# Slots 1 to 24 of a top-k attention kernel issued in an order from a table, with one small add as a tile and a load of v behind another transfer

## The chip, the cores and the metric

The kernel runs on one core of one Trainium2 chip. The metric is the time of one execution in microseconds (us), as the device measures it. A core has five engines with a queue of instructions each, worked off in order: TensorE (PE; its weight loads are shown apart as PEld), VectorE (DVE), ScalarE (ACT), GpSimd (POOL) and SyncE (SP), which here issues nearly all transfers between HBM and the on-chip memory SBUF. Queues wait for one another through semaphores, which the framework sets from the order in which the program issues its instructions.

## The reference

Attention over 8 batches, 8 heads, 576 tokens and head dimension 64, in which each row of scores keeps its 32 largest values, and then a feed-forward layer with a gated activation:

```
scores = scale * q @ k.T                      # per batch and head: 576 x 576
kth    = 32nd largest of each row
scores = where(scores >= kth, scores, -1e9)
attn   = exp(scores - max)
attn   = attn / (sum(attn) + 1e-9)
x      = attn @ v                             # (8*576) x 512 after joining the heads
h      = x @ w_in                             # 512 -> 2048
out    = (h * sigmoid(1.702 * h)) @ w_out     # 2048 -> 512
```

Inputs of the attention are float32; the two weights come as 64-bit floats and are rounded to float32 on the chip.

## The kernel before, in words

**Slots.** The attention is cut into 144 slots, 18 for each batch. A slot is 128 query rows of two heads: `scores` (L330) multiplies q and k on TensorE in tiles of 64x64; `copy_scores` (L345) brings one copy from the accumulators (PSUM) to SBUF on ScalarE (tile `sc`, four buffers); `pair_up` (L354) writes the larger and the smaller of each pair of scores on VectorE (L360), which frees the accumulators; `topk` (L374) finds the 32 largest by four rounds of MAX8 (L386) and three of MATCH_REPLACE8 (L390) per head on VectorE; `bounds` (L399) makes the cut and the offset on GpSimd; `mask` and `exps` (L418, L428) make the exponentials and their sums `den` on ScalarE; `invert` (L433) adds 1e-9 and takes the reciprocal `rden`. For slots up to 11 (`PAIRED`) the add is a scalar add on VectorE (L439), for later ones on GpSimd (L437).

**From weights to x.** Up to slot 9 the probabilities are turned by TensorE (`divide`, L448, and `turn`, L468 and L471). From slot 10 on `normalize` (L454, GpSimd) divides them, `split` (L490, ScalarE) separates their halves into the buffer `sc`, SyncE writes them to HBM (`rows`, L492) and a transposing transfer brings them back turned (`turn_by_dma`, L498). The next `copy_scores` that uses the same buffer must wait until `rows` is written. `values` and its variants (L526, L557, L586) multiply with v; the result is `x`.

**The feed-forward layer.** Four slots make a block of 128 tokens, 36 in all. A block has four units: `hidden` (L662, TensorE), `tanh` (L678 and L681, ScalarE), `gate` (L690, L691 on GpSimd; L693 on VectorE for the first two blocks), `combine` (L715 to L718, GpSimd) and `project` (L760 for the first two blocks, L776 after). For the first two blocks `hidden` and `project` use tiles of 128x128, after that of 128x64.

**Weights.** In slots 0 to 10 the 32 pieces of the weights are loaded into a ring of seven buffers (`load_piece`, L134) and rounded: ScalarE (L155, L157, L159), a shift on VectorE (L158, 32 times), and two or three passes on GpSimd (L148, L151, L156). The buffers are free for the next loads when the passes are done.

**What sets the order.** It is written out by hand: the program is issued line by line, and each engine works in that order. `opening` starts, `slot(n)` (L949) issues slots 0 to 10, `filling_slot` (L1099) slots 11 to 20, and `steady_pair` (L1175) two slots at a time from 21 on. In all of them a stage of slot n is issued beside later stages of slots before it: the scores of slot n + 2, the search of n, the exponentials of n - 1, the values of n - 2 or n - 3. `filling_slot` issues a `load_v` that is due (one, in slot 20: L210 and L221, the v of the second batch) ahead of the scores, so ahead of the `rows` of that slot on SyncE's queue.

Of the kernel before, what the change touches and what calls it, by code (L numbers as in the profile page):

```python
# [9 lines left out]
ALU = mybir.AluOpType  # L10
ENG = mybir.EngineType
F32 = mybir.dt.float32
# [7 lines left out]
P = 128  # L20
# [9 lines left out]
TO_ZERO = 2.0**-100  # L30


@with_exitstack
def kernel(
    ctx: ExitStack,
# [23 lines left out]

    nc = tc.nc

    B, H, S, D = q.shape
    C = H * D
# [24 lines left out]
    STEADY = PAIRED + 2  # L90
# [5 lines left out]
    const = ctx.enter_context(tc.tile_pool(name="const", bufs=1))  # L96
# [22 lines left out]
    make_identity(nc, ident[:])  # L119
    win = const.tile([P, CC, DFF], F32, name="win")  # L120
    wout = const.tile([P, FC, C], F32, name="wout")

# [170 lines left out]
    def write_all():  # L293
        while writes:
            writes.pop(0)()
# [26 lines left out]
    N = len(slots)  # L322
    PER = N // B
    st = [{} for _ in slots]
# [108 lines left out]
    def invert(n):  # L433

        some = small.tile([P, 2], F32, name="some", tag="sums")
        if n > PAIRED:
            nc.gpsimd.tensor_scalar(some[:], st[n]["den"][:], 1e-9, None, op0=ALU.add)  # L437
        else:
            nc.vector.tensor_scalar_add(some[:], st[n]["den"][:], 1e-9)  # L439
        rden = st[n]["rden"] = small.tile([P, 2], F32, name="rden", tag="inverse")  # L440
        nc.vector.reciprocal(rden[:], some[:])  # L441

# [402 lines left out]
    for n in by_slot:  # L845
        first = sum(map(len, list(by_slot.values())[:n]))
# [60 lines left out]
    def opening():  # L907

        stay_warm(8, v_tail[:, 0, :, :].rearrange("p j d -> p (j d)"))
        load("q", 0, 0, nc.sync)  # L910
        load("k", 0, 0, nc.scalar)
        for hp in range(2):
            for name in "qk":
                if hp:
                    load(name, 0, hp)
        for x in by_slot[0]:
            load_piece(x)
        prepare_first()
# [180 lines left out]
    def filling_slot(n, beside, pool_ahead, behind, pool_behind, late=[]):  # L1099

        todo = later.pop(n, [])
        due = [(fn, args) for fn, args in todo if fn is prepare_by_dma]
        exponentials(n - 1)
        for fn in beside:
            fn()
        for fn in pool_ahead:
            fn()
        find(n, 8)
        for fn, args in todo:
            if fn is load_v:  # L1110
                fn(*args)
        scores(n + 2)
        if n == PAIRED:
            normalize(n - 1)
            split(n - 1)
            copy_scores(n + 2)
        else:
            copy_scores(n + 2)
            normalize(n - 1)
            split(n - 1)  # L1120
        write_all()
        for fn, args in todo:
            if fn not in (prepare_by_dma, load_v):
                fn(*args)
        turn_by_dma(n - 1)
        while turns:
            turns.pop(0)()
        for fn in pool_behind:
            fn()
        bounds(n)  # L1130
        for fn in behind + late:
            fn()
        for fn, args in due:
            fn(*args)
# [106 lines left out]
    def last_units():  # L1241
# [7 lines left out]
        project_one()  # L1249
        leave_all()  # L1250

    with tc.manual_schedule():
# [41 lines left out]
```

## Time and profile before

| | |
|---|---|
| median of 3 runs | 1378.75 us (1377.12 to 1379.25) |
| the profiled execution | 1379.59 us |
| its span, first to last instruction | 1377.8 us |
| mean granted TensorE clock | 0.992 |

Busy time by engine and by stretches of the span, the chain that ended last, and the groups of instructions are views of the same execution. In a row of groups stand line, engine, operation, output and inputs with their shapes, the count, then the busy time and the mean of one instruction, then the idle time of the engine ahead of them with what ended it. A row of instructions in order of time begins with start and length in us. Idle time of an engine costs something only where that engine, or one that waits for it, sets the end.

### The profile page before, as it was taken

What the parts mean: (1) busy time and instruction counts of PE and PEld (TensorE: products, weight loads), DVE (VectorE), ACT (ScalarE), POOL (GpSimd) and SP (SyncE); (2) the same over time, 40 slices, a digit from 0 to 9 for tenths busy, and PEclk for the clock granted to TensorE, in tenths of its full rate; (3) what the DMA queues carried; (4) which work ended last, traced back from release to release, by engine and by line L of the source; (5) the groups of instructions that cost most, each with busy time, mean ns of one, the idle gap of its engine ahead of it and who ended that gap; (6) DMA issues with size and microseconds to landing.
All of it is one profiled execution on the core that took longest, in us unless ns stands there. A gap on an engine that the chain in (4) does not pass through costs nothing.

```text
span 1377.8 us, 54398 instructions
## 1 busy us (share of the span) xinstructions
PE 1341.2 (97%) x22560; PEld 1205.0 (87%) x22560; DVE 1286.0 (93%) x3392; ACT 1164.1 (84%) x1930; POOL 964.4 (70%) x1758
## 2 busy tenths in 40 slices
PE   7789999999999999999999999999999999999998
PEld 5676578899999999999999999999998999999998
DVE  7999998999999999999999999999999999999912
ACT  6988887998889888988898988888888998888841
POOL 3776676777777776777777777677777777777770
PEclk8999999999999999999999999999999999999999
DMA  7551568787889786977898668988888768855640
GB/s 232 155 163 62 151 159 198 179 196 196 205 210 211 178 189 173 232 193 192 192 227 208 182 174 193 210 198 191 197 211 208 195 176 183 184 142 135 151 118 17
DMA packets 527223, 246.92 MB, mean 179 GB/s; under 512 B 458880, under 2 KB 505472, under 8 KB 526976
## 3 DMA queue, kind: packets, MB, share of 16 engines
q1 hardware_dynamic: 526544, 243.16, 71.5%
q8 instruction: 177, 2.90, 0.9%
q14 instruction: 70, 0.57, 0.1%
q10 hardware_dynamic: 432, 0.30, 0.1%
HBM read 46.01 MB, written 103.42 MB: 108 GB/s over the span
## 4 chain that ended last, share of the span: by engine, by line
PE 79%; DMA 3%; ACT 1%; issue 0%; POOL 0%; SPq 0%; DVE 0%; DVEq 0%; ACTq 0%; POOLq 0%
PE ph L662 32%; PE po L776 28%; PE o L586 10%; PE s_ps L339 9%; DMA pt<-rows 2%; DMA rows<-sc 1%; ACT pr L428 0%; ACT sc L418 0%; ACT sc L490 0%; ACT sc L350 0%; ACT halves L268 0%; ACT raws L794 0%; SPq L221 0%; POOL pr L454 0%; ACT h L681 0%
## 5 line engine op out<-in xcount | busy, mean ns | idle before, releaser
L386 DVE MAX8 top<-ranked 128x8 f32<-128x288 f32 (+1 forms) x1152 | 637.6, 596 | 0.0
L662 PE MATMUL ph<-xT,win 128*64 128x128 f32 (+1 forms) x8544 | 493.8, 273 | 0.0
L662 PEld LDWEIGHTS ph<-xT,win 128*64 128x64 f32 (+1 forms) x8544 | 469.4, 137 | 27.6 <-issue 24.1
L390 DVE MATCH_REPLACE8 ranked<-top,ranked 128x288 f32<-128x288 f32 (+1 forms) x864 | 462.4, 543 | 0.0
L490 ACT COPY sc<-pr 128x2304 uint16<-128x2304 uint16 x134 | 283.4, 2115 | 90.1 <-POOL pr L454 90.0
L454 POOL TENSOR_SCALAR pr<-pr,rden 128x576 f32<-128x576 f32 x268 | 197.9, 748 | 49.2 <-DVE rden L441 47.7
L428 ACT ACTIVATE pr<-sc,low 128x576 f32<-128x576 f32 x288 | 219.9, 769 | 0.0
L418 ACT ACTIVATE sc<-sc,cut 128x576 f32<-128x576 f32 x288 | 208.6, 779 | 4.7 <-POOL cut L404 4.7
L360 DVE TENSOR_TENSOR ranked<-s_ps,sc 128x576 f32<-128x576 f32 x286 | 201.8, 747 | 3.8 <-ACT sc L350 3.8
L776 PE MATMUL po<-raws,h 128*64 128x128 f32 x2112 | 205.3, 273 | 0.0
L776 PE MATMUL po<-wout,h 128*64 128x128 f32 x2112 | 205.3, 273 | 0.0
L350 ACT COPY sc<-s_ps 128x576 f32<-128x576 f32 x286 | 168.5, 642 | 26.9 <-PE s_ps L339 14.4
L437 POOL TENSOR_SCALAR some<-den 128x2 f32<-128x2 f32 x132 | 29.3, 222 | 221.6 <-ACT pr L428 221.4
L339 PE MATMUL s_ps<-qk_t 64*64 64x288 f32 x2304 | 177.6, 421 | 5.6 <-DVE ranked L360 4.4
L691 POOL TENSOR_TENSOR th<-th,h 128x512 f32<-128x512 f32 x134 | 171.8, 1282 | 11.2
L776 PE MATMUL po<-wout,th 128*64 128x128 f32 x2176 | 165.3, 273 | 0.0
L776 PEld LDWEIGHTS po<-raws,h 128*64 128x64 f32 x2112 | 133.8, 137 | 0.0
L776 PEld LDWEIGHTS po<-wout,h 128*64 128x64 f32 x2112 | 133.7, 137 | 0.0
L776 PEld LDWEIGHTS po<-wout,th 128*64 128x64 f32 x2176 | 127.8, 137 | 0.9 <-POOL wout L739 0.4
L339 PEld LDWEIGHTS s_ps<-qk_t 64*64 64x64 f32 x2304 | 76.2, 134 | 58.1 <-issue 14.8
L586 PE MATMUL o<-pt,v_l 128*64 128x128 f32 (+1 forms) x2240 | 124.8, 265 | 0.0
L586 PEld LDWEIGHTS o<-pt,v_l 128*64 128x64 f32 x2240 | 110.3, 137 | 10.1 <-issue 9.5
(118 smaller groups left out, 1647.5 us busy)
## 6 DMA issues: line engine op xcount, KB each, us to landing
rows<-sc SPq DMA_DIRECT2D x134, 576.0 KB, 4.0
qk_rows<-halves SPq DMA_DIRECT2D x24, 576.0 KB, 5.5
out_dram<-raws SPq DMA_DIRECT2D x68, 128.0 KB, 3.7
raws<-in_moe_w_in_dram SPq DMA_DIRECT2D x16, 512.0 KB, 5.1
raws<-in_moe_w_out_dram SPq DMA_DIRECT2D x16, 512.0 KB, 3.7
qk_l<-in_q_dram SPq DMA_DIRECT2D x28, 256.0 KB, 4.4
qk_l<-in_k_dram SPq DMA_DIRECT2D x28, 256.0 KB, 4.2
v_l<-in_v_dram SPq DMA_DIRECT2D x4, 1024.0 KB, 8.8
```

The lines of the kernel that those rows point to most:

```text
L339: nc.tensor.matmul(ps[rows, i, c, 0:HALF], lhsT=qT[b, hps[p]][on, cols], rhs=kT[b, hps[p]][on, FIRST[i] + c * HALF : FIRST[i] + (c + 1) * ...
L360: nc.vector.tensor_tensor(out=ranked[n][:, :, c, :], in0=a, in1=b, op=op)
L386: nc.vector.max(top[:, i, 8 * r : 8 * r + 8], of(r, i))
L390: nc.vector.match_replace(to, top[:, i, 8 * r : 8 * r + 8], of(r, i), LOWEST)
L418: nc.scalar.activation(sc[:, i, :], sc[:, i, :], AF.Prelu, bias=cut[:, i : i + 1], scale=SCALE, alpha=HUGE)
L428: nc.scalar.activation(pr[:, i * S : (i + 1) * S], sc[:, i, :], AF.Exp, bias=low[:, i : i + 1], accum_out=den[:, i : i + 1],)
L454: nc.gpsimd.tensor_scalar(pr[:, i, :], pr[:, i, :], st[n]["rden"][:, i : i + 1], 1.0, op0=ALU.mult, op1=ALU.mult)
L490: nc.scalar.copy(out=halves, in_=pr[:].bitcast(U16).rearrange("p (k h) -> p h k", h=2))
L586: nc.tensor.matmul(o[s][j * D : (j + 1) * D, cols], lhsT=lhsT, rhs=rhs, start=(s, j) not in halves[:k], stop=(s, j) not in halves[k + 1 :],)
L662: nc.tensor.matmul(ph[rows, i * P : (i + 1) * P], lhsT=win[:, c, f * P + rows.start : f * P + rows.stop], rhs=xs[:, x.place, c, :], start= ...
L691: nc.gpsimd.tensor_tensor(out=th[:], in0=th[:], in1=h, op=ALU.mult)
L776: nc.tensor.matmul(both_banks[bank][y * TAIL : (y + 1) * TAIL, to * P : (to + 1) * P], lhsT=a[:, i, :], rhs=weight(w, fs[i])[:, y, :], sta ...
```

## The change: what it does

Three things. First, `nc` becomes an object that keeps the calls to the five engines in a list while `collected` is a list, in place of issuing them. `opening`, slots 0 to 20 and the pairs 21/22 and 23/24 are collected so, 2597 steps. A table of step numbers, `ORDER`, then says in which order they are issued (`a+n` stands for n steps from a on); each number occurs once. The rest of the program is issued as before. Buffers are given out when the calls are collected, so they are the same ones.

```diff
+COLLECTED = 25
+
+ORDER = """
+8 11 0+8 9 12 10 13+5 22 18 23+2 33 25+2 19 27+5 34 32 20 38+4 35 21 36 97 37 42+4 98 46+4 99 50 54+6 100 53 51
...
+2489 2596 2532+2 2592 2568+8 2490 2591 2534+2 2594 2491 2593 2522+2 2536+2 2524+2 2492+2 2587+2
+"""
...
+        def step(*args, **kwargs):
+            if self.engines.collected is None:
+                do(*args, **kwargs)
+            else:
+                self.engines.collected.append(lambda: do(*args, **kwargs))
...
-    nc = tc.nc
+    nc = Engines(tc.nc)
...
     with tc.manual_schedule():
+        nc.collected = []
         opening()
         for n in range(SETTLED + 1):
             slot(n)
         filling()
-        for n in range(STEADY + 8, N + 2, 2):
+        for n in range(STEADY + 8, COLLECTED, 2):
+            steady_pair(n)
+        issue_in_order()
+        for n in range(COLLECTED, N + 2, 2):
             steady_pair(n)
```

Counted by engine, 1392 of the steps are TensorE's, 480 VectorE's, 351 ScalarE's, 249 GpSimd's and 125 SyncE's. Set against the hand-written order, the step at a given place of the queue is another at 1241, 411, 284, 219 and 4 places. Up to the search of slot 0 VectorE's order is the same. From slot 1 on searches of two slots alternate on VectorE, the weight shifts stand in 19 groups (11 before), pieces of `hidden`, `project` and `values` alternate on TensorE, copies of scores stand ahead of exponentials on ScalarE, and the sums of weights (L739) stand earlier on GpSimd. The eight products of one slot's scores stand together from slot 8 on, and the shape of TensorE's tiles changes 107 times (83 before).

Second, the 1e-9 of the slots up to 11 is kept in a tile, and the add on VectorE is one of two tiles.

```diff
+    little = const.tile([P, 2], F32, name="little")
+    nc.gpsimd.memset(little[:], 1e-9)
...
-            nc.vector.tensor_scalar_add(some[:], st[n]["den"][:], 1e-9)
+            nc.vector.tensor_tensor(out=some[:], in0=st[n]["den"][:], in1=little[:], op=ALU.add)
```

Third, a due `load_v` in `filling_slot` is issued with the other loads, behind `write_all()` and the `rows` of the slot before. On SyncE's queue these are the four changed places: the three transfers of v and the `rows` that they now follow.

```diff
         find(n, 8)
-        for fn, args in todo:
-            if fn is load_v:
-                fn(*args)
         scores(n + 2)
...
         write_all()
         for fn, args in todo:
-            if fn not in (prepare_by_dma, load_v):
+            if fn is not prepare_by_dma:
                 fn(*args)
```

More of the change, by code (lines that the diff above doesn't have):

```diff
@@ L30, with __init__, __getattr__ @@
 TO_ZERO = 2.0**-100
+COLLECTED = 25
+ORDER = """
[83 rows of a table added]
+"""
+class Engine:
+    def __init__(self, engines, engine):
+        self.engines, self.engine = engines, engine
+    def __getattr__(self, name):
+        do = getattr(self.engine, name)
+        def step(*args, **kwargs):
[3 more added lines that the diff above has]
+                self.engines.collected.append(lambda: do(*args, **kwargs))
+        return step
+class Engines:
+    def __init__(self, nc):
+        self.collected = None
+        for name in ("tensor", "vector", "scalar", "gpsimd", "sync"):
+            setattr(self, name, Engine(self, getattr(nc, name)))
 @with_exitstack
@@ L118 @@
     ident = const.tile([P, P], F32, name="ident")
-    make_identity(nc, ident[:])
+    make_identity(tc.nc, ident[:])
+    little = const.tile([P, 2], F32, name="little")
+    nc.gpsimd.memset(little[:], 1e-9)
     win = const.tile([P, CC, DFF], F32, name="win")
@@ L1250, in last_units, with issue_in_order @@
         leave_all()
+    def issue_in_order():
+        steps, nc.collected = nc.collected, None
+        order = list(range(len(steps)))
+        if ORDER.split():
+            order = []
+            for part in ORDER.split():
+                first, _, count = part.partition("+")
+                order += range(int(first), int(first) + int(count or 1))
+        assert sorted(order) == list(range(len(steps)))
+        for i in order:
+            steps[i]()
     with tc.manual_schedule():
+        nc.collected = []
         opening()
```

81 rows, old and new, of the table ORDER are left out of this document.

## The prediction

> **What bounds the kernel now.** I read the page first, then the busy time by stretches of 50 us, then the chain of waits, and last the waits of VectorE up to 250 us, the end of the part that the table covers.
>
> ```profile
> span 1377.8 us, 54398 instructions
> PE 1341.2 (97%) x22560; PEld 1205.0 (87%) x22560; DVE 1286.0 (93%) x3392; ACT 1164.1 (84%) x1930; POOL 964.4 (70%) x1758
> ```
>
> Two engines are nearly full over the span, so the stretches decide (columns: stretch, then busy us and instructions of TensorE, its weight loads, VectorE, ScalarE and GpSimd, then granted clock, DMA share and GB/s).
>
> ```profile
> 50.00:100.00 50.00, 44.28 (x454) 38.81 (x452) 48.74 (x127) 44.88 (x85) 36.52 (x45) 0.98 0.53 160
> 100.00:150.00 50.00, 46.20 (x368) 33.95 (x367) 46.94 (x119) 41.35 (x78) 33.38 (x41) 0.97 0.24 77
> 150.00:200.00 50.00, 46.27 (x491) 31.08 (x491) 48.59 (x132) 42.71 (x78) 38.25 (x56) 1.00 0.67 166
> 200.00:250.00 50.00, 47.13 (x896) 43.04 (x894) 44.69 (x117) 41.10 (x67) 34.12 (x63) 1.00 0.81 195
> 250.00:300.00 50.00, 50.00 (x888) 45.53 (x886) 50.00 (x137) 44.48 (x72) 36.91 (x70) 1.00 0.80 184
> 400.00:450.00 50.00, 50.00 (x888) 45.53 (x884) 49.22 (x133) 45.89 (x72) 36.74 (x71) 1.00 0.88 214
> ```
>
> From 250 us on TensorE has no idle time, and VectorE a little. The chain says the same: it lies on DMA and ScalarE until 243.02 us and then on TensorE without a break (columns: start, length, what).
>
> ```profile
> 228.76 8.15 DMA rows<-sc
> 243.02 2.46 PE o L586 x76
> 256.81 3.06 PE po L776 x56
> 259.87 1.13 PE s_ps L339 x16
> 424.82 3.49 PE ph L662 x64
> 428.32 1.13 PE s_ps L339 x16
> 429.45 3.65 PE ph L662 x64
> 442.45 3.49 PE ph L662 x64
> ```
>
> A steady pair of slots takes TensorE 442.45 − 424.82 = 17.63 us. VectorE needs less: with no wait it begins the pairing of the next slot (L360) every 8.63 us, 17.26 us a pair.
>
> ```profile
> 15.17 1.42 DVE L360 TENSOR_TENSOR ranked<-s_ps,sc 128x576 f32<-128x576 f32 x2 [0.24 <-ACT sc L350]
> 256.66 1.41 DVE L360 TENSOR_TENSOR ranked<-s_ps,sc 128x576 f32<-128x576 f32 x2
> 265.29 1.41 DVE L360 TENSOR_TENSOR ranked<-s_ps,sc 128x576 f32<-128x576 f32 x2
> ```
>
> So the steady part, untouched by the change, starts about 263 us and its length is set by TensorE's queue. Whatever TensorE gains or loses before that is kept to the end, as long as VectorE keeps step. How far VectorE may fall behind can be read here: the pairing for slot 25 ends at 256.66 + 1.41 = 258.07 us, and the scores that wait for it (those of slot 26) begin at 259.87 us, so it has 1.8 us to spare.
>
> **The change part by part.** The same 2597 steps are issued, so the sum is over idle time and over instructions that last longer than they need. Decoding the table, I find that the pairing for slot 1 and the one for slot 25 have the same places in VectorE's order before and after (instructions of the program 16 and 471 of 480). Between them stands the same work. VectorE's part therefore moves by exactly what its waits and overlong instructions between 15.17 and 256.66 us change.
>
> Its waits up to 250 us (columns: who waits, for whom, us in total, times, longest):
>
> ```profile
> DVE some L439 <- ACT pr L428: 4.2, 8, 1.1
> DVE rden L441 <- POOL some L437: 3.7, 4, 1.2
> DVE ranked L360 <- ACT sc L350: 3.2, 2, 3.0
> ```
>
> *v behind rows.* Two of these waits are one event. In slot 20 the queue of SyncE issues the loads of v ahead of the probabilities (rows) of slot 19:
>
> ```profile
> 226.58 0.59 SPq L210 DMA_DIRECT2D v_l<-in_v_dram  x1
> 228.76 1.14 SPq L492 DMA_DIRECT2D rows<-sc  x1
> rows<-sc SPq DMA_DIRECT2D x134, 576.0 KB, 4.0
> v_l<-in_v_dram SPq DMA_DIRECT2D x4, 1024.0 KB, 8.8
> 237.00 1.18 ACT L350 COPY sc<-s_ps 128x576 f32<-128x576 f32 x2 [4.63 <-DMA rows<-sc]
> 238.22 1.42 DVE L360 TENSOR_TENSOR ranked<-s_ps,sc 128x576 f32<-128x576 f32 x2 [2.99 <-ACT sc L350]
> 241.37 0.17 DVE L441 RECIPROCAL rden<-some 128x2 f32<-128x2 f32 x1 [1.07 <-POOL some L437]
> 240.06 1.20 PE L339 MATMUL s_ps<-qk_t 64*64 64x288 f32 x16
> ```
>
> The rows wait 228.76 − 226.58 = 2.18 us for their turn, then take 8.15 us instead of the usual 4.0 because they share the DMA engines with 1 MB of v. The score buffer that they read comes free late, ScalarE stands 4.63 us and VectorE 2.99 + 1.07 = 4.06 us. Issued first, the rows should land about 226.58 + 4.0 = 230.6 us, before ScalarE would ask (237.00 − 4.63 = 232.4 us). The wait is gone: 4.06 us for VectorE. For TensorE it is less, for its next bound is its own queue: the scores ahead of the values at 243.02 us run until 240.06 + 1.20 = 241.26 us, so those values come at most 1.8 us earlier. Late next is v itself: issued one instruction (1.14 us) later, and with the usual 8.8 us, it lands at 226.58 + 1.14 + 8.8 = 236.5 us, still ahead of the values that need it.
>
> *The order.* The other waits make 4.2 + (3.7 − 1.07) + (3.2 − 2.99) = 7.0 us. In the table the waiting instruction (add or reciprocal) is moved behind one to five searches of another slot, and the score copies are issued ahead of the exponentials on ScalarE. I count two thirds of the 7.0 us as regained, 4.7 us; the bounds are 0 and 7.0. New waits can arise in any in-order queue; they are the third kept back, and the rivals.
>
> TensorE must gain as well. Its idle time from 100 to 250 us is 3.80 + 3.73 + 2.87 = 10.4 us, from the stretches above. The table fills it with pieces of the hidden layer and the projection, of later slots. From the third block of tokens on all of those have 128x64 tiles, and so have most of the values. Tile shapes alternate more often than before in slots up to 11 (77 times for 51) and as often behind (30 for 32). A change of shape is dear where a group of 64 follows scores: 3.65 us for 3.49 in the chain, 0.16 us. Twenty-six more of them make 4.2 us, in slots whose TensorE stood idle for 5.7 us from 50 to 100 us alone; that idle time is the cover, and without it the price would be the 4.2 us. [...]
>
> *1e-9 as a tile.* Twelve adds, on VectorE, of slots up to 11:
>
> ```profile
> L439 DVE TENSOR_SCALAR some<-den 128x2 f32<-128x2 f32 x12 | 7.0, 582 | 4.2 <-ACT pr L428 4.2
> 55.34 1.29 DVE L439 TENSOR_SCALAR some<-den 128x2 f32<-128x2 f32 x1 [0.43 <-ACT pr L428]
> 55.27 1.34 POOL L148 TENSOR_SCALAR raws<-raws 128x512 f16<-128x512 f32 x1
> 56.67 0.17 DVE L441 RECIPROCAL rden<-some 128x2 f32<-128x2 f32 x1
> 56.69 0.69 POOL L156 TENSOR_SCALAR win<-raws 128x512 f32<-128x512 f32 x1
> 1355.81 0.75 DVE L715 TENSOR_TENSOR sums<-th 128x128 f32<-128x128 f32 x1 [1.27 <-PE po L776]
> 1355.68 0.73 POOL L798 TENSOR_TENSOR raws<-raws 128x256 f32<-128x256 f32 x1 [18.23 <-ACT raws L794]
> 1361.09 0.29 DVE L715 TENSOR_TENSOR sums<-th 128x128 f32<-128x128 f32 x1
> ```
>
> The add of 1.29 us ends at 56.63 us, just behind GpSimd's pass, which ends at 56.61. The reciprocal, of the same size and with GpSimd busy beside it, takes 0.17 us. So the adds hold 7.0 − 12 × 0.17 = 5.0 us of waiting for GpSimd. Does an add of two tiles wait too? The reciprocal's row says no (gain 5.0 us), but it has one input; the last three rows show an add of two SBUF tiles that takes 0.75 us instead of 0.29 and ends (1356.56) behind GpSimd's 1356.41. That is the nearest, so I take 0, and keep 5.0 as the upper end and −5.0 (twice the waiting) as the lower. [...]
>
> *Shifts of the weights.* 32 of them, in 11 groups before, stand in 19 groups in the table. A group met by a GpSimd pass is longer:
>
> ```profile
> 28.48 1.08 DVE L158 TENSOR_SCALAR win<-win 128x512 uint32<-128x512 uint32 x3
> 38.66 1.86 DVE L158 TENSOR_SCALAR win<-win 128x512 uint32<-128x512 uint32 x3
> ```
>
> 0.78 us is the dearest seen. Eight more groups at half of it cost 3.1 us; the bounds are 0 and 19 × 0.78 = 14.8 us.
>
> *The sum.* VectorE: 4.06 + 4.7 + 0 − 3.1 = 5.7 us earlier. TensorE may use that and the 1.8 us of slack, 7.5 us, which is 72% of its idle time. I take the middle of 5.7 and 7.5, 6.6 us. The profiled execution took 1379.59 us (span 1377.8); less 6.6 that is 1373.0, and the median of the runs shown lies 0.84 us below the profiled one, so 1372.2 us.
>
> **The rivals.** *Both engines are packed.* All waits go (4.06 + 7.0), the adds are freed (5.0) and the shifts cost nothing more: VectorE 16.1 us. TensorE can follow by its 10.4 us and by what VectorE gains ahead of 100 us, where seven of the twelve adds lie (7/12 × 5.0 = 2.9 us), 13.3 us in all: 1379.59 − 13.3 − 0.84 = 1365.4 us. For it: both idle sums are there. Against it: TensorE's steady stretch is without idle time, but here it waits for results of all other engines.
>
> *Only v counts.* The waits move to other instructions of the same queues, and 1.8 us of TensorE remain: 1379.59 − 1.8 − 0.84 = 1376.9 us, within 0.2% (2.8 us, about what a measurement of this kernel can tell from no change). For it: GpSimd and ScalarE are 73% and 90% busy from 50 to 100 us, and every moved step is in one in-order queue with them.
>
> *Slower: shifts that meet GpSimd.* Place: VectorE in slots 2 to 11, whose lost time TensorE cannot make up. If each of the 19 groups pays the dearest price, the shifts cost 14.8 us; VectorE ends 14.8 − 4.06 − 4.7 = 6.0 us later, TensorE, less its 1.8 us, 4.2 us: 1379.59 + 4.2 − 0.84 = 1383.0 us. It decides from (4.06 + 4.7 + 1.8) / 19 = 0.56 us a group. For it: GpSimd is busy 36.52 of 50 us there, and the table fills its gaps. Against it: the group at 28.48 us paid nothing.
>
> **How the numbers follow.** The forecast (gain 3 to 10 us) gets 0.55; both engines packed 0.13; only v 0.16; slower 0.16, of which 0.02 stays within 0.2%. Faster by over 0.2% is below 1376 us: 0.55 + 0.13 + 0.01 of the v case = 0.69. Within 0.2%: 0.15 + 0.02 = 0.17. Slower: 0.14. The range goes from the packed case, 1364, to between no change and the slower case, 1381 us; the forecast's own range is 1369 to 1376.
>
> **What would show it.** v: the wait of ScalarE's score copy for rows near 232 us is gone, and rows land in about 4 us. Order: the pairing for slot 25 starts near 251 us instead of 256.66, and the stretches 100 to 250 us show TensorE idle for 3 to 5 us instead of 10.4. Adds: L439's successor still has a mean near 582 ns and ends with GpSimd's passes; at 0.17 us each my zero is wrong. Shifts: the sum of their times grows by about 3 us. The forecast falls if the steady pair's 17.63 us changes, if pairing 25 moves and TensorE's chain does not, or if a new wait of over 2 us appears ahead of slot 24.

## The result, and the profile after

| | before | after |
|---|---|---|
| time, median of the runs (range), us | 1378.16 (1377.12 to 1379.25) | 1371.55 (1370.43 to 1374.03) |
| ratio to before, 95% interval | | 0.9956 [0.9941, 0.9971] |
| profiled execution (span), us | 1379.59 (1377.8) | 1372.24 (1370.5) |
| first steady projection, TensorE, us | 263.11 | 255.98 |
| pairing for slot 25 begins, VectorE, us | 256.66 | 246.27 |

The kernel became 6.6 us faster by the medians, 6.1 us (4.0 to 8.1) by the ratio. All instructions are now issued through a helper, so that the rows carry L133 (collected and reordered) or L131 (issued directly), and one reads by tiles.

The first view is the chain of waits of the changed kernel (start, length, what).

```profile
222.37 4.10 DMA rows<-sc
226.49 8.14 DMA pt<-rows
234.87 2.60 PE o L133 x80
...
251.42 1.13 PE s_ps L133 x16
...
255.98 3.06 PE po L131 x56
```

From 255.98 us on the chain lies on TensorE and is the one of the kernel before, which had the same `po` group at 263.11 us: 7.13 us earlier, and the span is 7.3 us shorter. So the whole gain was made ahead of that place. There TensorE is the later of the two: VectorE's pairing that ends at 247.7 us was needed at 251.42 us only.

The busy time by stretches shows where TensorE is idle now (columns as in the prediction).

```profile
50.00:100.00 50.00, 46.77 (x430) 36.41 (x429) 47.60 (x128) 46.31 (x92) 35.38 (x46) 0.97 0.49 144
100.00:150.00 50.00, 49.22 (x370) 35.03 (x367) 50.00 (x135) 43.36 (x77) 40.36 (x48) 1.00 0.30 97
150.00:200.00 50.00, 46.91 (x589) 33.88 (x590) 48.89 (x132) 44.58 (x83) 41.34 (x61) 1.00 0.75 184
200.00:250.00 50.00, 47.77 (x908) 43.61 (x906) 48.05 (x128) 44.43 (x71) 33.71 (x67) 1.00 0.87 190
```

TensorE's idle time in these four stretches was 5.72 + 3.80 + 3.73 + 2.87 = 16.1 us and is 3.23 + 0.78 + 3.09 + 2.23 = 9.3 us. These are equal times, not equal work. Up to its first steady projection TensorE has the same 2724 instructions behind it in both kernels (first the kernel before, then the changed one):

```profile
0.00:263.11 263.11, 233.73 (x2724) 185.93 (x2726) 243.44 (x635) 217.67 (x395) 176.72 (x259) 0.96 0.59 161
0.00:255.98 255.98, 239.90 (x2724) 187.36 (x2726) 241.10 (x645) 220.36 (x398) 178.22 (x263) 0.97 0.62 165
```

Its idle time ahead of that place fell from 29.4 to 16.1 us, by 13.3 us, and nearly half of that lies in the first 50 us, where TensorE was busy for 36.74 us before and is for 43.25 us now. But the same instructions are busy for 239.90 us in place of 233.73, although the mean granted clock is no lower (0.97 for 0.96). So the 7.1 us are 13.3 us less idle time and 6.2 us more busy time. What makes the work longer, changes of tile shape or short gaps that the view counts as busy, no run here separates.

For VectorE, the stretch from the pairing for slot 1 to that for slot 25, first of the kernel before, then of the changed one:

```profile
15.17:256.66 241.49, 213.51 (x2488) 168.97 (x2490) 230.16 (x599) 205.01 (x372) 171.33 (x242) 0.96 0.58 160
```

```profile
15.43:246.27 230.84, 216.44 (x2428) 167.17 (x2430) 224.80 (x600) 203.44 (x370) 169.82 (x239) 0.97 0.61 163
```

It became 10.65 us shorter with the same work between: VectorE's idle time fell from 11.33 to 6.04 us, and its busy time (VectorE's column) from 230.16 to 224.80. Of those 5.36 us the adds give 2.6 and the shifts of the weights 1.0; the rest is not in any one group. The groups, before and after (the shifts of `wout` went from 5.8 to 6.1 us):

```profile
L158 DVE TENSOR_SCALAR win<-win 128x512 uint32<-128x512 uint32 x16 | 7.4, 511 | 0.0
```

```profile
L133 DVE TENSOR_SCALAR win<-win 128x512 uint32<-128x512 uint32 x16 | 6.1, 412 | 0.0
L133 DVE TENSOR_TENSOR some<-den,little 128x2 f32<-128x2 f32 x12 | 4.4, 367 | 0.7 <-ACT pr L133 0.7
```

Its two longest waits in that stretch (a third, of the adds for the exponentials, is 0.7 us), and two of the waits of other engines up to 250 us:

```profile
DVE ranked L133 <- ACT sc L133: 4.1, 5, 1.7
DVE rden L133 <- POOL some L133: 1.2, 1, 1.2
```

```profile
POOL win L133 <- DVE win L133: 10.3, 6, 2.5
PE o L133 <- DMA pt<-rows: 3.9, 3, 1.7
```

Three kinds of wait of 11.1 us became 6.0 us. GpSimd now waits for the shifts of the weights, for which it did not wait before, and VectorE's waits for GpSimd fell from 3.7 to 1.2 us. TensorE's wait for `pt` is the one that stands in the chain. SyncE's queue shows where it comes from (start, length of the issue):

```profile
222.37 0.35 SPq L133 DMA_DIRECT2D rows<-sc  x1
222.77 0.43 SPq L133 DMA_DIRECT2D v_l<-in_v_dram  x1
...
226.49 4.57 SPq L133 DMA_TRANSPOSE pt<-rows  x1
```

The rows of slot 19 now go first and land at 226.47 us; ScalarE's wait for them fell from 4.63 to 0.74 us:

```profile
226.57 1.18 ACT L133 COPY sc<-s_ps 128x576 f32<-128x576 f32 x2 [0.74 <-DMA rows<-sc]
```

Over the whole part up to 250 us ScalarE still waits 3.7 us for rows, in three pieces (4.6 us in one piece before). And the transposing transfer behind them shares its time with v (which landed at 231.20 us) and takes 8.14 us; in the kernel before, where the rows were the late ones, it took 4.78 (236.92 to 241.70 us).

### The profile page after: what moved, and what is told of

It is laid out like the page before. It is cut to its first block, busy times and chain, and to the rows that moved or that the text cites. A ratio compares the mean times of both kernels' runs of the same rounds, so it can differ in the third digit from the quotient of the medians.

```text
span 1370.5 us, 54397 instructions
## 1 busy us (share of the span) xinstructions
PE 1347.7 (98%) x22560; PEld 1206.7 (88%) x22560; DVE 1280.4 (93%) x3392; ACT 1165.1 (85%) x1930; POOL 964.5 (70%) x1759
## 4 chain that ended last, share of the span: by engine, by line
PE 81%; DMA 2%; ACT 1%; SPq 0%; issue 0%; DVE 0%; DVEq 0%; ACTq 0%
PE ph L131 32%; PE po L131 28%; PE o L131 10%; PE s_ps L131 9%; DMA pt<-rows 1%; DMA rows<-sc 1%; PE po L133 1%; PE ph L133 1%; PE o L133 0%; SPq L131 0%; ACT sc L133 0%; PE s_ps L133 0%; ACT sc L131 0%; ACT pr L131 0%; ACT h L131 0%
## 5 line engine op out<-in xcount | busy, mean ns | idle before, releaser
L131 DVE MAX8 top<-ranked 128x8 f32<-128x288 f32 (+1 forms) x952 | 526.6, 595 | 0.0
L131 PE MATMUL ph<-xT,win 128*64 128x128 f32 x8064 | 464.2, 273 | 0.0
L131 PEld LDWEIGHTS ph<-xT,win 128*64 128x64 f32 x8064 | 441.2, 137 | 25.9 <-issue 22.8
L131 DVE MATCH_REPLACE8 ranked<-top,ranked 128x288 f32<-128x288 f32 x714 | 382.0, 543 | 0.0
L131 ACT COPY sc<-pr 128x2304 uint16<-128x2304 uint16 x120 | 253.6, 2114 | 86.7 <-POOL pr L131 86.7
L131 POOL TENSOR_SCALAR pr<-pr,rden 128x576 f32<-128x576 f32 x240 | 177.3, 750 | 39.7 <-DVE rden L131 39.7
L131 PE MATMUL po<-wout,h 128*64 128x128 f32 x2000 | 194.2, 273 | 0.0
L131 PE MATMUL po<-raws,h 128*64 128x128 f32 x2000 | 194.2, 273 | 0.0
L131 ACT ACTIVATE pr<-sc,low 128x576 f32<-128x576 f32 x240 | 183.2, 769 | 0.0
L131 ACT ACTIVATE sc<-sc,cut 128x576 f32<-128x576 f32 x240 | 174.0, 780 | 0.1
L131 POOL TENSOR_SCALAR some<-den 128x2 f32<-128x2 f32 x120 | 26.7, 222 | 206.6 <-ACT pr L131 206.6
L131 DVE TENSOR_TENSOR ranked<-s_ps,sc 128x576 f32<-128x576 f32 x236 | 166.6, 747 | 1.9 <-ACT sc L131 1.9
L131 POOL TENSOR_TENSOR th<-th,h 128x512 f32<-128x512 f32 x123 | 157.8, 1283 | 10.3
L131 PE MATMUL po<-wout,th 128*64 128x128 f32 x2064 | 156.6, 273 | 0.0
L131 ACT COPY sc<-s_ps 128x576 f32<-128x576 f32 x234 | 138.0, 642 | 17.9 <-PE s_ps L131 10.2
L131 PE MATMUL s_ps<-qk_t 64*64 64x288 f32 x1872 | 140.5, 415 | 0.0
L131 PEld LDWEIGHTS po<-raws,h 128*64 128x64 f32 x2000 | 126.4, 137 | 0.0
L131 PEld LDWEIGHTS po<-wout,h 128*64 128x64 f32 x2000 | 126.4, 137 | 0.0
L131 PEld LDWEIGHTS po<-wout,th 128*64 128x64 f32 x2064 | 121.3, 137 | 0.0
L131 PE MATMUL o<-pt,v_l 128*64 128x128 f32 (+1 forms) x2144 | 120.7, 266 | 0.0
L131 PEld LDWEIGHTS o<-pt,v_l 128*64 128x64 f32 x2144 | 106.6, 137 | 9.9 <-issue 9.1
L131 POOL TENSOR_TENSOR h<-th 128x128 f32<-128x128 f32 x248 | 114.0, 460 | 0.3
## 6 DMA issues: line engine op xcount, KB each, us to landing
out_dram<-raws SPq DMA_DIRECT2D x68, 128.0 KB, 3.5
```

The lines of the kernel that those rows point to most:

```text
L131: do(*args, **kwargs)
```

## The experiments

All ratios are to the kernel before, measured beside the run. The changed kernel stands at 0.9956 [0.9941, 0.9971].

### One part alone: v behind the rows

```diff
         for fn, args in todo:
-            if fn is load_v:
-                fn(*args)
...
-            if fn not in (prepare_by_dma, load_v):
+            if fn is not prepare_by_dma:
```

> The kernel before with one part of the change: v is issued behind the rows of a slot; the order of the slots and the scalar add stay as they were. My theory (TensorE's arrival at the steady pairs sets the time, a wait of VectorE counts only as far as TensorE has it too): VectorE's score copy no longer waits for the rows of slot 19 (2.99 and 1.07 us go), the transposing transfer behind the rows shares its time with v and takes some 8 us instead of under 5, and the time falls by 0 to 2 us, to 1376 to 1378. Rival one, VectorE's wait counts in full: 4 us less, 1374. Rival two, the transposing transfer that v now slows costs as much as the wait: no change, or up to 2 us more.

Measured: 1376.67 us, ratio 0.9984 [0.9973, 0.9994], a gain of 2.2 us (0.8 to 3.7). VectorE's pairing that waited 2.99 us for the score copy begins with no wait, 8.78 us behind the one ahead of it, and the next one follows after 8.62 us:

```profile
234.69 1.41 DVE L360 TENSOR_TENSOR ranked<-s_ps,sc 128x576 f32<-128x576 f32 x2
```

The transposing transfer took 8.74 us here too (229.72 to 238.46), but TensorE, later than in the changed kernel, asked for it at 241.91 us only. The gain fits the 1.8 us of TensorE's slack; a wait that counts in full (4 us) lies just outside the interval. VectorE did not keep all of its gain: at 247.67 us a reciprocal waits 2.27 us for GpSimd, so that the pairing for slot 25 begins only 2.3 us earlier than before (254.32 us).

### One part alone: the add as a tile

```diff
...
-            nc.vector.tensor_scalar_add(some[:], st[n]["den"][:], 1e-9)
+            nc.vector.tensor_tensor(out=some[:], in0=st[n]["den"][:], in1=little[:], op=ALU.add)
```

> The kernel before with one part of the change: 1e-9 of single slots is added as a tile on VectorE. My theory (it is the place of the add that makes it long, beside GpSimd's pass, and not the form of its second operand): the twelve adds of the first 24 slots stay near a mean of 0.58 us (sum 7 us), and the time stays within 1 us of the kernel before. Rival, the tile's form is what shortens them: the mean falls to 0.37 us or lower (sum 4.4 us or less), and the time by up to 2 us.

### The change without the tile

```diff
-            nc.vector.tensor_tensor(out=some[:], in0=st[n]["den"][:], in1=little[:], op=ALU.add)
+            nc.vector.tensor_scalar_add(some[:], st[n]["den"][:], 1e-9)
```

> The changed kernel with one part taken back: 1e-9 is added as a number again, the order and the place of v stay. My theory: VectorE comes 3.7 us early to the steady pairs in the changed kernel, so that even adds longer by 2.6 us in sum leave the time within 0.7 us of the changed kernel's. Rival, VectorE's time counts: 1 to 3 us more than the changed kernel.

Measured: the tile alone 1378.48 us, ratio 1.0003 [0.9991, 1.0014]; the change without it 1371.48 us, 0.9947 [0.9932, 0.9963]. The adds, first of the tile in the old order, then of the number in the new one:

```profile
L441 DVE TENSOR_TENSOR some<-den,little 128x2 f32<-128x2 f32 x12 | 5.8, 483 | 3.4 <-ACT pr L430 3.4
```

```profile
L133 DVE TENSOR_SCALAR some<-den 128x2 f32<-128x2 f32 x12 | 5.2, 431 | 0.6 <-ACT pr L133 0.5
```

With a number the twelve took 7.0 us in the kernel before and 5.3 in the run with v alone, in the same order; with the tile 5.8. In the new order they took 5.2 with a number and 4.4 with the tile. The 483 ns fell between what the two theories expected, and in the old order the two forms differ by less than the number's own two runs do. For the time the form is worth nothing that was measured. Nor does the tile keep an add short beside GpSimd: in the changed kernel the add at 42.12 us, with GpSimd idle, took 0.16 us, and the one at 97.49 us took 1.17 us and ended at 98.66 us, GpSimd's pass of 1.30 us beside it at 98.64.

### The change with v ahead of the rows

```diff
+        for i in (2049, 2050, 2051):          # the three transfers of v
+            order.remove(i)
+        at_rows = order.index(2048)           # the rows of slot 19
+        order[at_rows:at_rows] = [2049, 2050, 2051]
```

> The changed kernel with the three transfers of v put back ahead of the transfer of slot 19's rows on SyncE's queue; nothing else of the order is changed. Theory one (the rows come late as in the kernel before, all engines wait for them): the steady chain starts 2 to 4 us later than in the changed kernel and the time is 1373 to 1376. Theory two (v costs the transposing transfer behind the rows as much as it costs the rows): within 1 us of the changed kernel.

Measured: 1378.17 us, ratio 0.9988 [0.9974, 1.0002]. The new order with v ahead keeps at most 3.6 us of the gain, and v's place is worth 6.7 us by the medians, 5.7 by the ratios, against the run without the tile, which ran beside it (1371.48): more than either theory gave and over twice the 2.2 us of the old order. Up to slot 22 nothing is lost: its pairing begins at 216.6 us (changed kernel 217.2, before 226.4). Then the rows come late, and TensorE's queue shows what that costs now; first this kernel, then the changed one:

```profile
234.86 2.20 PE L133 MATMUL s_ps<-qk_t 64*64 64x288 f32 x16 [3.62 <-DVE ranked L133]
...
238.49 3.23 PE L133 MATMUL o<-pt,v_l 128*64 128x64 f32 x64
```

```profile
232.26 1.20 PE L133 MATMUL s_ps<-qk_t 64*64 64x288 f32 x16
234.87 0.59 PE L133 MATMUL o<-pt,v_e 64*64 64x64 f32 x16 [1.41 <-DMA pt<-rows]
235.39 2.08 PE L133 MATMUL o<-pt,v_l 128*64 128x64 f32 x64
```

TensorE could begin these scores at 231.2 us (the kernel before began them at 240.06), so it stands idle for 3.62 us, and then the same groups take 2.20 and 3.23 us in place of 1.20 and 2.08. The stretch gives the reason, the granted clock (third figure from the end), which is 1.00 in the same stretch of the changed kernel:

```profile
236.00:240.00 4.00, 3.49 (x56) 2.44 (x50) 4.00 (x15) 3.08 (x7) 3.17 (x5) 0.50 0.04 15
```

So this wait of 3.62 us cost its own length, and behind it the granted clock was 0.55 from 234 to 236 us, 0.50 to 240 us and 0.74 to 242 us. The profiled execution of the run without the tile (1376.13 us, the longest of its six; the median is 1371.48) had the same on a smaller scale: its transposing transfer took 9.98 us, TensorE waited 2.65 us for it, and the granted clock was 0.50 from 238 to 240 us.

```profile
236.18 0.59 PE L133 MATMUL o<-pt,v_e 64*64 64x64 f32 x16 [2.65 <-DMA pt<-rows]
```

### Half of the table

```diff
+        order = [i for i in order if i < 1204] + list(range(1204, len(steps)))    # table to slot 11
```

> The changed kernel, with the order of the table for slots 1 to 11 only; from slot 12 on the steps run in the order in which the program gives them, with v behind the rows as there. In the profiles, TensorE's idle time of the stretch 50 to 150 us is 9.5 us before and 4.0 us after, that of 150 to 250 us 6.6 and 5.3. Theory one (what TensorE gains early stays gained, and v gives 2 us as it does alone): some 5.5 us and 2 us, 1371 to 1373, as the changed kernel. Theory two (the early gain is lost again before the steady pairs, in waits for transfers, since the transfers of slots 17 to 20 come at the same time whatever stood before them): only v's 2 us remain, 1376 to 1377.

```diff
+        order = list(range(1204)) + [i for i in order if i >= 1204]    # table from slot 12
```

> The changed kernel, with the order of the table from slot 12 on only; slots 1 to 11 run in the order in which the program gives them. Theory one (the early idle time of TensorE is what the table saves): v's 2 us and 0 to 1.5 us more, 1375 to 1377. Theory two (the table's later part sets when the transfers start, and so the time): 1371 to 1373, as the changed kernel.

Measured: 1381.93 us, ratio 1.0022 [1.0010, 1.0034], and 1379.81 us, 1.0010 [0.9998, 1.0021]. Both theories of both runs missed: each half is no faster than the kernel before, though both have v behind the rows. In the first the pairing for slot 12 begins at 128.4 us (changed kernel 128.0), and then the cut itself costs about 8 us (slot 13 at 147.4 us, there 137.2; some 2 us of the 10 are six VectorE instructions that stand ahead of this pairing here and behind it in the table). Its waits from 100 to 150 us:

```profile
PE s_ps L133 <- DVE ranked L133: 8.1, 1, 8.1
DVE wout L133 <- POOL wout L133: 6.7, 1, 6.7
```

A shift of the weights on VectorE waits for GpSimd's piece of it, searches and pairings stand behind it in VectorE's queue, and TensorE's scores wait for the pairing. So this run prices the cut. In the second no wait of that size stands near the cut (TensorE's longest there is 1.95 us, at 147.00 us); VectorE's pairing for slot 25 begins 3.7 us earlier than before, and why its time does not show that stays open. So does the time of a half.

For VectorE alone a division can be read off where pairings begin that have the same work ahead of them in both orders. That holds for slots 1, 17 and 25:

| VectorE, us | slot 1 to 17 | slot 17 to 25 |
|---|---|---|
| before | 180.80 − 15.17 = 165.6 | 256.66 − 180.80 = 75.9 |
| v alone | 180.34 − 15.17 = 165.2 | 254.32 − 180.34 = 74.0 |
| changed | 173.86 − 15.43 = 158.4 | 246.27 − 173.86 = 72.4 |
| table from slot 12 | 180.98 − 14.66 = 166.3 | 252.94 − 180.98 = 72.0 |

```profile
180.80 1.41 DVE L360 TENSOR_TENSOR ranked<-s_ps,sc 128x576 f32<-128x576 f32 x2
```

```profile
173.86 1.41 DVE L133 TENSOR_TENSOR ranked<-s_ps,sc 128x576 f32<-128x576 f32 x2
246.27 1.42 DVE L133 TENSOR_TENSOR ranked<-s_ps,sc 128x576 f32<-128x576 f32 x2
```

Of VectorE's 10.65 us the order made 7.2 us ahead of slot 17. Behind it came 3.5 us, of which v alone gives 1.9.

### v further ahead, and no v at all

```diff
+        for i in (2049, 2050, 2051, 1901):    # v, and the transposing transfer of q and k
+            order.remove(i)
+        behind = order.index(2009) + 1        # last product that reads the old v
+        order[behind:behind] = [2049, 2050, 2051]
+        order.insert(order.index(2223) + 1, 1901)    # behind the rows of slot 20
```

> The changed kernel, with the three transfers of v moved ahead on SyncE's queue, to right behind the last product that reads the old v, and the transposing transfer of q and k that stood there moved behind the rows of slot 20, ahead of whose scores nobody reads it. Theory one (v's megabyte is what stretches the transposing transfer of slot 19 to 8.1 us, and TensorE's 1.41 us and ScalarE's waits for it are the chain's next link): that transfer takes 4.5 to 5.5 us, and the time falls by 1 to 2.5 us more, to 1369 to 1370.5. Theory two (it is the engines' own work that comes next): within 0.7 us of the changed kernel. Against both: rows of slot 19 that now share their time with v's end come later, and the time rises by 1 to 4 us.

```diff
+        order = [i for i in order if i not in (2049, 2050, 2051)]
```

> The changed kernel without the three transfers of v that stand behind the rows of slot 19 (left out altogether: the products of the third batch read the v of the second, nothing else changes). This bounds what any place of v can bring. Theory one: the transposing transfer of slot 19 falls from 8.1 us to 4.5 to 5.5 us, and the time by 1.5 to 3 us. Theory two (v is hidden behind the rows): within 0.7 us of the changed kernel.

Measured: 1373.16 us, ratio 0.9957 [0.9945, 0.9970] with v ahead; 1368.87 us, 0.9923 [0.9910, 0.9936] without it. With v ahead the transposing transfer took 4.71 us, as expected, but now the rows share with v:

```profile
221.72 6.52 DMA rows<-sc
...
235.62 3.93 PE o L133 x78
```

They take 6.52 us, TensorE waits 0.95, 0.81 and 0.66 us within 4 us, and the granted clock is 0.50 from 236 to 238 us (3.93 us for the products, 2.60 in the changed kernel). In the kernel without v the three transfers are left out, so that the second batch, from slot 18 on, reads the v of the first (the expectation names the third and the second, one too far). There the transposing transfer takes 5.93 us, a little over what I expected. By the medians v costs this place 2.7 to 4.3 us (1368.87 against 1371.55 and, in the same set of runs, 1373.16) wherever it is put among these transfers: it moves the delay from one to the other. Part of that may be TensorE's clock: three of the six executions without v had a mean granted clock of 0.998, which no execution of the other two kernels had. The three at 0.994 and 0.995 took 1369.52 to 1370.27 us, 1.4 us less than the changed kernel and 2.9 less than the one with v ahead, by the medians of the executions at those clocks.

### VectorE given more to do

```diff
-            nc.vector.max(top[:, i, 8 * r : 8 * r + 8], of(r, i))
+            for _ in range(5 if n == 26 and r == 0 and i == 0 else 1):
+                nc.vector.max(top[:, i, 8 * r : 8 * r + 8], of(r, i))
```

> The changed kernel with four more repeats of one search instruction on VectorE in slot 26 (some 3.0 us of VectorE's time; they write the same values). In the changed kernel VectorE has slot 26's scores in hand 3.7 us after it could begin. Theory one (TensorE's arrival sets the time and VectorE has that much to spare): within 0.7 us of the changed kernel. Theory two (VectorE's time counts in full, as in the kernel before by the share of its busy time): 3 us more, 1374.5.

Measured: 1372.85 us, ratio 0.9952 [0.9935, 0.9969]. By the ratio that is the changed kernel's time; the medians of the two, from different sets of runs, differ by 1.3 us. The four repeats took 2.0 us, not the 3.0 of the expectation: in the trace they are searches of 288 values, one every 0.5 us. 2.0 us in full would be 0.9970, at the edge of the interval, so the time alone hardly excludes that they count. The trace does for its execution: behind them TensorE has no idle time.

```profile
250.00:300.00 50.00, 50.00 (x888) 45.53 (x886) 48.93 (x130) 44.97 (x71) 35.15 (x67) 1.00 0.82 192
```

So 2 us of VectorE's lead of 3.7 us are not what the gain rests on. The trace has one more reading for the clock: TensorE waited 1.98 us for `pt` here, the granted clock was 1.00 from 234 to 240 us, and the products behind it took 2.09 us.

```profile
235.07 0.68 PE L133 MATMUL o<-pt,v_e 64*64 64x64 f32 x16 [1.98 <-DMA pt<-rows]
```

### The idle time filled

v stands ahead of the rows as above, and besides (`outs` holds accumulators of the values):

```diff
...
         for i in order:
+            if i == 2292:                     # the scores of slot 24
+                for _ in range(16):
+                    nc.tensor.matmul(outs[0][:, 0:P], lhsT=ident[:], rhs=ident[:], start=True, stop=True)
             steps[i]()
```

> The kernel with the new order and v ahead of the rows of slot 19 (1378.17 us), in which TensorE stood idle for 3.62 us ahead of the scores of slot 24 and then had half the clock: sixteen products of the identity with itself, whose result is overwritten, are put into that idle time. The rows come as late as there, only the idle time is filled. Theory one (the half clock is a good part of what v costs in that place: the scores took 2.20 us for 1.20, the products of values 3.23 for 2.08): the clock stays at 1.00 and the time falls by 1.5 to 3 us, to 1375 to 1376.7. Theory two (it is the wait itself): no change, or up to 1 us more.

Measured: 1382.86 us, ratio 1.0019 [1.0006, 1.0033]. A miss that tells nothing about its question: the products had to wait for the accumulators that they write.

```profile
238.16 5.46 PE L131 MATMUL o<-ident 128*128 128x128 f32 x32 [4.57 <-ACT h L133]
```

They did not fill the idle time; they began behind it. How the 6 us or so of v ahead divide between wait and clock is read from the rows above only: 2.15 us of longer groups, 1.00 for the scores and 1.15 for the values.

### The next link taken out

```diff
+        first, second = [2300, 2301, 2304, 2305, *range(2308, 2324)], [2302, 2303, 2306, 2307, *range(2324, 2340)]
+        places = sorted(order.index(i) for i in first + second)
+        for place, i in zip(places, first + second):    # values of slot 18, then of slot 19
+            order[place] = i
```

> The changed kernel, with the forty products of values of slots 18 and 19 reordered: those of slot 18 first, whose transposed rows lie there by 221.5 us, then those of slot 19, for whose rows TensorE waited 1.41 us in the changed kernel (2.65 us in the run with the scalar add, after which its clock was granted at 0.50 and the products took 3.94 us in place of 2.60). Theory one (that wait and the half clock that follows it where it is long are the next thing in TensorE's way): the wait goes, two more changes of tile shape cost some 0.3 us, and the time falls by 0.7 to 2 us against the changed kernel, to 1369.5 to 1371, with fewer runs above 1373. Theory two (what is won there is lost in the next wait): within 0.7 us of it.

The last run adds to this:

```diff
+        order.remove(1901)                              # transposing transfer of q and k
+        order.insert(order.index(2223) + 1, 1901)       # behind the rows of slot 20
```

> The changed kernel with two edits: the products of slot 18 ahead of those of slot 19, as in the run before (ratio to the kernel before 0.9944), and the transposing transfer of q and k that stands ahead of slot 19's rows, whose result nobody reads before the steady pairs, moved behind the rows of slot 20. Theory one (the transfers of slot 19 share their time with it: the rows take 4.10 us in the changed kernel and 2.9 to 3.0 where nothing else moves): the rows of slot 19 take 3.0 to 3.5 us, the whole stretch from their issue to slot 19's transposed rows 10.5 to 11.5 us in place of 12.25, and the ratio to the kernel before falls to 0.9935 or lower. Theory two (v's megabyte and the engines' own work decide): the ratio stays between 0.994 and 0.996. Against both: the transfer that is moved now stretches the transposed rows of slot 20, and the time rises by up to 2 us.

Measured: 1372.07 us, ratio 0.9944 [0.9923, 0.9965] for the first, which can't be told from the changed kernel; TensorE's wait fell from 1.41 to 0.67 us, and what it waits for is ScalarE (`h`). For the second 1368.85 us, 0.9923 [0.9911, 0.9935], below the changed kernel's interval. Its chain and TensorE's queue:

```profile
220.08 3.60 DMA rows<-sc
...
252.90 3.06 PE po L131 x56
```

```profile
230.98 0.40 PE L133 MATMUL o<-pt,v_e 64*64 64x64 f32 x8
...
232.39 0.45 PE L133 MATMUL o<-pt,v_e 64*64 64x64 f32 x8
```

TensorE goes from the scores to the values of both slots without a wait, and the chain no longer passes through `pt`. The rows took 3.60 us and the stretch to the transposed rows 11.86 us, each a little over what I expected, while the transposing transfer itself stayed at 8.25 us: what was taken away is who waits for it.

How much of the 2.7 us the two edits win is open. Four of the six executions, the profiled one among them, had a mean granted clock of 0.997 or 0.998; none of the changed kernel's four was above 0.995. These four took 2.3 us less, in the mean, than the two at 0.994 (1369.81 and 1371.61 us). In the traces the difference in clock lies in the first 100 us, where both kernels have the same order:

```profile
0.00:50.00 50.00, 42.26 (x348) 31.68 (x348) 41.30 (x114) 37.24 (x74) 22.69 (x36) 0.97 0.70 208
```

There it is 0.97, and 1.00 from 50 to 100 us; in the changed kernel it is 0.90 and 0.97. The profiled execution leads ahead of the moved transfers already: the transposing transfer of slot 18 was issued at 212.52 us, in the changed kernel at 214.13, 1.6 of the 3.1 us by which its steady projection begins earlier.

## Why the prediction was right, and where it was not

**The bound.** Right. The steady pair stayed at 17.63 us, what moved is TensorE's start (7.13 us), and VectorE's 2 us more did not delay TensorE. But the prediction had TensorE held by what VectorE gains (5.7 us and 1.8 of slack); VectorE gained 10.4 us, and TensorE's 7.1 were set by `pt` and its own queue.

**v behind rows.** TensorE's 1.8 us are right for v alone (2.2, 0.8 to 3.7). "Late next is v itself" is the step that failed: v landed at 231.2 us, ahead of the products of slots 18 and 19 that need it at 234.87 us, and late is the transposing transfer of the same slot, which v stretches from 4.78 to 8.14 us. The prediction counted v's transfer against the rows ahead of it, and not against the `pt` behind it on the same queue. In the new order v's place is also worth more than 1.8 us, some 6 us, because TensorE arrives earlier and the granted clock was 0.50 behind its wait of 3.62 us; the two parts' gains don't simply add (0.9988 and 0.9984 alone, 0.9956 together, though the intervals would still allow a sum).

**The order.** The mechanism is right, the sizes are not. Waits: 8.8 us were to go with v's, 5.1 went, since the pairing now waits 4.1 us for the score copy. TensorE's idle time from 100 to 250 us was to fall to 3 to 5 us and fell to 6.1; the stretch from 50 to 100 us, which the prediction used as cover only, gave 2.5 us, and the first 50 us, which it left out, gave more (6.5 us). On the other side the same work became 6.2 us longer on TensorE. The prediction priced 26 more changes of shape at 4.2 us and let idle time cover them; whether the 6.2 us are theirs is open, but that the new order costs TensorE nothing can't be said.

**1e-9 as a tile.** Zero was right for the time, by two runs. The reason given (it waits for GpSimd like the add of a number) fits the add of 1.17 us beside GpSimd's pass; that the mean would stay near 582 ns does not: it fell to 367 ns. That new places shorten the adds is shown for the tile (483 ns in the old order; 367 in the changed kernel, 317 in the run with v ahead of the rows). With the number it is not: 431 ns in the new order, 446 and 582 in the old one.

**Shifts.** Not borne out. More groups were to cost 3.1 us; the sum fell from 13.2 to 12.2 us (13.1 in the run without v, which has the same groups). The prediction priced a group as if it met a GpSimd pass as often as before; in the table it is GpSimd that waits (10.3 us for `win`).

**The sum.** VectorE's 5.7 us were 10.65. Its waits gave 3.7 us less than counted, the shorter adds, shifts and other instructions 8.5 us more than the −3.1 taken. The total was still right, 6.6 for 6.6 us by the medians, but that agreement is luck in good part: the 6.6 were the middle between VectorE's 5.7 us and 7.5 us with the slack, VectorE was not what held TensorE back, and TensorE's own sum was another one, 13.3 us less idle time and 6.2 us more work.

**The rivals.** Both packed: VectorE made 10.4 of its 16.1 us, and TensorE, stopped by `pt` and by its own longer work, 7.1 of the 13.3 us that this rival gave it; 1365.4 us was not reached. Only v counts: excluded, 1376.9 us is v alone. Slower by shifts: excluded. **The signs.** Pairing 25 moved further than the 251 us named, the wait for rows near 232 us is down to 0.74 us, and the rows took 4.10 us: nearly as forecast. That "a new wait of over 2 us appears ahead of slot 24" was to make the forecast fall. One did appear, and the forecast stood: at 54.66 us TensorE waits 2.41 us for VectorE's pairing, where the kernel before has no such wait.

```profile
54.66 0.67 PE L133 MATMUL s_ps<-qk_t 64*64 64x288 f32 x2 [2.41 <-DVE ranked L133]
```

So that sign was too strict for a part in which TensorE has idle time to lose. Where it has none, the wait for `pt` was 1.41 us in the profiled execution and 2.65 us in one of the run without the tile, which took 4.65 us more than its median.

**Open.** What each half of the table gives in time; how much of the early gain is TensorE's clock (below); what makes TensorE's work 6.2 us longer; how much of the last run's lead is clock; and the share of the clock in v's price, since the idle time could not be filled.

## What to carry to other kernels

Where a large load has to pass between two small transfers that are chained, moving it ahead of or behind one of them only chose, here, which of the two is late. What took the wait away was to let the consumer do first what does not need the late one (the other slot's products) and to move a third transfer, whose result nobody reads yet; how much time that saves is open. An order that brings one engine forward can raise the price of a delay behind it (v's place: 2.2 us in the old order, some 6 in the new one), so that a cheap wait of the old order is to be priced again in the new one. Idle time that an order fills is not all gain: count the busy time of the same instructions as well. And to cut an order in two does not measure its halves when the cut has a price of its own.

## What the runs showed of the hardware

TensorE's granted clock fell to 0.50 behind an idle time of 2.17 us in the kernel before, at 102.56 us, and of 2.65 us in the run without the tile, at 236.18 us:

```profile
102.56 2.88 PE L468 MATMUL tp<-by,pr 128*128 128x128 f32 x16 [2.17 <-POOL by L448]
```

```profile
102.00:104.00 2.00, 1.44 (x11) 1.44 (x12) 2.00 (x4) 1.54 (x4) 2.00 (x4) 0.89 0.49 197
104.00:106.00 2.00, 2.00 (x12) 1.45 (x11) 2.00 (x6) 0.87 (x2) 1.38 (x2) 0.50 0.30 55
106.00:108.00 2.00, 2.00 (x26) 1.10 (x26) 2.00 (x6) 1.93 (x5) 0.00 (x0) 0.75 0.98 342
```

```profile
236.00:238.00 2.00, 1.82 (x46) 1.78 (x47) 2.00 (x4) 0.54 (x1) 2.00 (x3) 0.76 0.36 147
238.00:240.00 2.00, 2.00 (x42) 2.00 (x41) 1.22 (x3) 0.91 (x3) 2.00 (x7) 0.50 0.09 20
240.00:242.00 2.00, 2.00 (x38) 2.00 (x36) 2.00 (x6) 1.82 (x2) 1.80 (x5) 0.88 1.13 247
```

The clock missing in the three windows is 2 × (0.11 + 0.50 + 0.25) = 1.72 us in the one and 2 × (0.24 + 0.50 + 0.12) = 1.72 us in the other: 3.44 us each time, if it was at the 0.50 of the middle window throughout. The length of the wait alone does not decide: 3.53 us at 91.83 us of the kernel before and 2.19 us at 177.08 us of the last run cost no clock (1.00 from 88 to 102 us and from 174 to 182 us),

```profile
91.83 2.05 PE L468 MATMUL tp<-by,pr 128*128 128x128 f32 x16 [3.53 <-POOL by L448]
92.00:94.00 2.00, 2.00 (x20) 1.88 (x20) 2.00 (x6) 0.67 (x2) 2.00 (x3) 1.00 0.11 43
```

```profile
177.08 1.09 PE L133 MATMUL o<-pt,v_l 128*64 128x128 f32 x16 [2.19 <-DMA pt<-rows]
178.00:180.00 2.00, 2.00 (x36) 1.37 (x32) 2.00 (x7) 0.91 (x4) 0.93 (x4) 1.00 0.03 7
```

and neither did 1.98 us above. What sets these waits apart from the two above, no run here shows.

So some of the order's gain may be clock. In the five stretches of 50 us up to 250 us the clock was 0.85, 0.98, 0.97, 1.00 and 1.00 before and is 0.90, 0.97, 1.00, 1.00 and 1.00 in the changed kernel: 10.0 and 6.5 us of full clock are missing. Three of the four executions in the old early order (before, v alone, the table from slot 12; not the tile alone) have a stretch of 2 us at a clock of 0.50 between 90 and 108 us, and none of nine in the table's early order has. But seven of those nine have one of 0.50 to 0.56 between 52 and 62 us, in the changed kernel (0.50 from 56 to 58 us) behind the wait of 2.41 us at 54.66 us. The run with v further ahead and the last run have none.

The transposing transfer of one slot took 4.71 us (v further ahead) and 4.78 us (the kernel before) with v out of its way, 5.93 us without v behind the new order, and beside v's megabyte 7.34 us (VectorE given more to do), 7.38 (the table from slot 12), 8.14 (the changed kernel) and 9.98 us (the run without the tile). That spread of 2.6 us is nearly twice TensorE's wait for it in the changed kernel (1.41 us).
